# Row tiles of the first token group in two runs of three, and low parts one product later, in a one-core attention, MLP and mixture kernel

## The chip, the cores and the metric

One core of a Trainium2 chip runs the whole program. The metric is the device time of one execution in microseconds (us). Engine names are those of the profile: PE is TensorE's matmul side, PEld its weight loads, DVE is VectorE, ACT is ScalarE, POOL is GpSimd, and SP issues the transfers.

## What is computed

Attention between 4 x 8 heads of 512 tokens and 32 state rows makes 2176 rows of 512 numbers. A leaky MLP follows (512 to 2048 to 512), and then eight experts, all of them applied to all rows and weighted by a matrix P, which a softmax over the gate and eight normalisations of rows and columns make:

```python
P = np.exp(logits - logits.max())
for _ in range(8):
    P /= P.sum(1, keepdims=True) + 1e-09
    P /= P.sum(0, keepdims=True) + 1e-09
    P *= N / E
for e in range(E):
    h = np.maximum(x @ w1[e], 0.0)
    ye = h @ w2[e]
    out += P[:, e:e + 1] * ye
```

Everything is float32. A float32 product is made of three fp32r products: high by high, high by low and low by high part.

## The kernel before

The change lies in the experts. `experts()` walks through 97 stages `s`: three token groups (768, 768 and 640 rows) times 32 units of 256 hidden columns (8 experts of 4 units), and one stage more to finish. In the first group, stage `s` makes two things.

The first is the first expert layer of unit `s`, as one level of Strassen's method: seven products, in the order m1, m6, m5, m7, m2, m4, m3 (the list that `quad` returns). Each is six matmuls of 128x384 into one of three PSUM banks, which the profile calls px (m1, then m2 on top), py (m6, then m7 and m4 on top) and pz (m5, then m3 on top). The banks come from a pool of three, so the next stage's m1, m6 and m5 write where this stage's px, py and pz were read. After m1, ACT copies px to p1. DVE adds (L956) make u2 from m6, u3 and c22 from m7, c21 from m4 and c12 from m3; c11 is px itself after m2. From each of the four results ACT makes a rectified high part (`g2h`, L971), and DVE the low part from the result and that high part (`g2l`, L972).

The second is the second expert layer of unit `s - 1`: six plain row tiles T0 to T5 of 128 tokens (`layer2_moe`), each six matmuls of 128x512 (L1267) into one of three banks, which DVE adds to the output rows, weighted by P (L1291; L1280 and L1285 in the first expert). T0 to T2 read the high and low parts of c11 and c21, T3 to T5 those of c22 and c12.

Every engine runs its instructions in the order in which this code issues them: the order of PE, DVE, ACT and SP in this part is the order of the text (`manual_schedule`). Other work comes in between at fixed places. `slot()` stands behind each product and each tile and lets the lanes advance: the splits of the next weights (ACT and POOL), the sums of the second layer's weights, which later groups need and which are written to DRAM (`sums_b`: L786, L789, L791, L794 on DVE, then two high parts L891 on ACT and two low parts L893 on DVE), the same sums of six units whose time is not at their own stage (lane "apart", input `rwl`), and the sums of the next group's rows (L697). `point()` counts places, and some lanes advance at listed counts (`PLACES`). In stages 1 to 5 the lane "gate" makes the normalisations of P: a chain of nine small DVE instructions (L513 to L516, L504 to L508) and a small PE product (pcs, L511), by turns.

`experts()` is also where the low parts are put: `relu` does not issue them, but appends them to the list `later`. Before the change a tile T follows product `min(T + lag, 6)`, with lag 1 (3 in stage 1), and `later` is emptied behind a tile's DVE instruction, from product 2 on (those of stage 0 behind the second product of stage 1).

Of the kernel before, what the change touches and what calls it, by code (L numbers as in the profile page):

```python
# [92 lines left out]
def body(ctx: ExitStack, tc: tile.TileContext, xt_in, xn_in, stb, stk, wd, ws, alpha, wgate, out):  # L93
# [589 lines left out]
    def sums_of(g):  # L683

        b11, b21, b12, b22 = blocks_of(g)
        t = {}
        homes = {1: (("T1 T2", "xl3"), ("T3", "xh4"), ("T4", "xl4")), 2: (("T1 T2", "xh4"), ("T3 T4", "xl4"))}
        for names, tag in homes[g]:
            names = names.split()
            rest = big.tile([P, len(names), 2, CH[2 * g][1]], F32, tag=tag, name=f"s{tag}_{g}")  # L690
            t |= {x: rest[:, i] for i, x in enumerate(names)}
        sum_t[g] = t
        for out, x, y in (
            (t["T1"], b12, b11), (t["T2"], b22, t["T1"]), (t["T3"], b22, b12), (t["T4"], b21, t["T2"])
        ):
            for k in range(2):
                nc.vector.tensor_tensor(out=out[:, k], in0=x[:, k], in1=y[:, k], op=ALU.subtract)  # L697
                yield 6
# [31 lines left out]
    def forms_in(made, names):  # L730
        for name in names.split():
            lanes["sums" if name in ("T1", "T2", "T4") else "blocks"].append(made[name])
# [64 lines left out]
    def weights_a(s):  # L797

        u = s % U2
        wa = [wp.tile([P, 3, FU], F32R, tag=f"wa{x}", name=f"wa{x}_{s}") for x in "hl"]  # L800
        wsum = [wp.tile([P, 4, FU], F32R, tag=f"ws{x}", name=f"ws{x}_{s}") for x in "hl"]
        pairs = [[w[:, i:i + 2, :] for w in wsum] for i in (0, 2)]
        name_left(left, s, wa, pairs)
        if s >= U2:
            for x, w, t in zip("hl", wa, wsum, strict=True):
                again(("a", x, u), w)
                again(("as", x, u), t)
            return
        t = raw2["a", s]
        if s == 0:  # L810
            sums = rawp.tile([P, 4, FU], F32, tag="raw", name=f"sum{s}")
        else:
            sums = p2["t"].tile([P, 4, FU], F32, tag="y", name=f"sum{s}", bufs=1)
        make = sums_left(nc.gpsimd, sums, *(t[:, i, :] for i in range(4)))
        yield next(make)
        split2(*wa, t[:, 0:3, :])
        for x, w in zip("hl", wa, strict=True):
            keep(("a", x, u), 0, 3, w)
        yield next(make) + 1
        split2(*pairs[0], sums[:, 0:2, :])  # L820
        yield 1
        split2(*pairs[1], sums[:, 2:4, :])
        for x, w in zip("hl", wsum, strict=True):
            keep(("as", x, u), 0, 4, w)
        if "raw" in p2:
            load_a(s + 1, p2["raw"])
        yield 1
# [86 lines left out]
    def apart():  # L914

        load_apart(None)
        yield 16
        for u in APART:
            yield from sums_b(u, raw_apart[u], "xl4", 4, 14)
# [247 lines left out]
    def finish(g):  # L1167

        yield 20
        yield from combine(g, nc.gpsimd, 14)  # L1170
        for h in range(2):
            for t0, nt in cuts(g, h):
                ps = rows(g, h, t0, nt)
                yield 1
                t = const.tile([P, DM], F32, tag="lt", name=f"row{g}_{h}_{t0}", bufs=1)
                nc.scalar.activation(out=t[:nt], in_=ps[:nt], func=AF.Copy)
                store(g, h, t0, nt, t)
                yield 5
# [56 lines left out]
    def spread_p():  # L1235

        for g in range(1, NG):
            t0, nt = GT[g]
            row = const.tile([E, 2 * CH[0][1]], F32, tag="lt", name=f"prow{g}", bufs=1)
            for i in range(0, nt, 3):  # L1240
                k = min(3, nt - i)
                ps = ps_a.tile([E, 512], F32, tag="a", name=f"ppr{g}_{i}")
                for j in range(k):
                    nc.tensor.transpose(ps[:, j * P:(j + 1) * P], pr[:, t0 + i + j, :], ident)
                yield 1
                nc.scalar.activation(out=row[:, i * P:(i + k) * P], in_=ps[:, :k * P], func=AF.Copy)
                yield 1
            spread[g] = dram.tile([E, 2 * CH[2 * g][1]], F32, tag=f"spread{g}", name=f"spread{g}")
            nc.sync.dma_start(out=spread[g], in_=row[:, :nt * P])
            yield 4  # L1250

    def load_p(g, e):

        n = 2 * CH[2 * g][1]
        nc.sync.dma_start(out=pb[:, e % 2, :n], in_=spread[g][e:e + 1, :].to_broadcast([P, n]))
# [48 lines left out]
    later, soon, lanes = [], [], {"gate": [], "early": [], "sums": [], "blocks": [], "w": [], "w2": [], "apart": [], "spread": [], "h": [], "out": []}  # L1304
    wait = dict.fromkeys(lanes, 0)

    def advance(lane):

        q = lanes[lane]
        while q:  # L1310
            try:
                wait[lane] = next(q[0]) - 1
                return True
            except StopIteration:
                q.pop(0)
        return False
# [4 lines left out]
    def point():  # L1321
        points[0] += 1
        for lane, at in at_point.items():
            while at and at[0] <= points[0] and advance(lane):
                at.pop(0)
# [22 lines left out]
    def flush(lane):  # L1348
        while advance(lane):
            pass  # L1350
        wait[lane] = 0
# [94 lines left out]
    def experts():  # L1446

        nonlocal pb, pool_order
        after = ["B11", "T2", "T1", "T3", "B21", "T4", "B22"]
        for s in range(NS2 + 1):  # L1450
            mults = quad(s) if s < NS2 else []
            plain = range(GT[0][1]) if 1 <= s <= U2 else []
            if s == UE + 2:
                lanes["apart"].append(apart())
            if s == U2 // 2:
                lanes["spread"].append(spread_p())
            if s == U2 - 5:
                flush("apart")
            if s % U2 == (U2 - 5 if s < U2 else U2 - 6) and s + U2 < NS2:
                lanes["early"].append(sums_of(s // U2 + 1))  # L1460
            if s % U2 == U2 - 1:
                flush("early")
                flush("spread")
            if s == U2:
                pool_order = tc.manual_schedule(engines={mybir.EngineType.Pool})
                pool_order.__enter__()
            if s == U2 + 1:
                banks.close()
                p2["m"] = ctx.enter_context(tc.tile_pool(name="ps_m", bufs=2, space=PSUM))
                p2["tr"] = ctx.enter_context(tc.tile_pool(name="ps_t", bufs=1, space=PSUM))  # L1470
            if s + 1 < NS2:
                lanes["w"].append(weights_a(s + 1))
            if s < NS2:
                lanes["w2" if s > 1 else "w"].append(weights_b(s))
            made = forms(s // U2 + 1) if s % U2 == U2 - 1 and s + 1 < NS2 else None
            if U2 < s < NS2:
                lanes["h"].append(sums2(s - 1))
            if s == 2 * U2 + 1:
                lanes["out"].append(finish(1))

            lag = 3 if s == 1 else 1

            for i in range(7):
                if i == 3 and s == U2 - 1:
                    pb = big.tile([P, 2, 768], F32, tag="xl5", name="pb")
                if i == 3 and s % UE == UE - 1 and U2 - 1 <= s < NS2 - 1:
                    load_p((s + 1) // U2, (s + 1) % U2 // UE)
                if mults:
                    point()
                    mults[i]()  # L1490
                    if made:
                        forms_in(made, after[i])
                    if i == 1:
                        while later:
                            later.pop(0)()
                    slot()
                for t in plain:
                    if min(t + lag, 6) == i:
                        point()
                        layer2_moe(s - 1, t)  # L1500
                        while later and i > 1:
                            later.pop(0)()
                        slot()
                if U2 < s < NS2:
                    product(s - 1, i)
                    slot()
            for lane in ("w", "w2", "sums", "blocks"):
                flush(lane)
        flush("out")
        finish_last(NG - 1)  # L1510
        pool_order.__exit__(None, None, None)
# [66 lines left out]
```

## Time and profile before

| What | Value |
|---|---|
| device time, median of 3 runs | 1783.4 us (1783.14 to 1783.88) |
| span of the profiled execution, first to last instruction | 1781.5 us |
| PE busy in the span | 1755.4 us, 99% |
| DVE busy in the span | 1511.1 us, 85% |
| POOL, ACT busy in the span | 1254.5 us, 714.5 us |
| granted TensorE clock, mean | 0.998 of full speed |

The span is the profiled execution's own time; what lies around it shows only in the runs' median, which is 1.9 us more. A share is a mean over stages with different limits, so the stretch of the first token group (about 403 to 908 us) is read by itself below. A busy PE is a modelled figure: matmuls are pipelined, and what tells a full PE from a waiting one is the distance from one matmul's start to the next one's.

### The profile page before, as it was taken

The numbers are of one execution on the slowest core, as the hardware profiler recorded it, in microseconds if no ns is written. First come the engines' busy times: TensorE is split into PE (matmuls) and PEld (weight loads), VectorE is DVE, ScalarE is ACT, GpSimd is POOL, SyncE is SP. The second block draws the span as 40 slices with busy tenths as digits, with TensorE's granted clock in tenths as the row PEclk, the third lists the DMA queues.
The fourth block names the chain that finished last, engine by engine and source line by source line (L and its number), as shares of the span: only waits on it lengthen the run. The fifth ranks groups of instructions, "written<-read, shape, count | busy, mean of one in ns | idle before, by whom it ended". The sixth has DMA issues, their size and how long they took to land.

```text
span 1781.5 us, 28789 instructions
## 1 busy us (share of the span) xinstructions
PE 1755.4 (99%) x9963; PEld 1637.0 (92%) x9963; DVE 1511.1 (85%) x2349; ACT 714.5 (40%) x1350; POOL 1254.5 (70%) x1288
## 2 busy tenths in 40 slices
PE   8999999999999999999999999999999999999998
PEld 8888888878888888888899999999998999999998
DVE  7879878778999999999977777777888888778877
ACT  7747667553334444443422222222223323233332
POOL 4536546577588777778657777777777897677775
PEclk9999999999999999999999999999999999999999
DMA  6212111227688999988877776777776887888884
GB/s 219 83 54 72 36 59 48 77 86 251 213 320 305 341 343 334 345 322 295 324 287 260 263 258 254 263 265 263 255 263 237 308 300 286 308 321 294 308 313 155
DMA packets 153009, 427.18 MB, mean 240 GB/s; under 512 B 17296, under 2 KB 34192, under 8 KB 152864
## 3 DMA queue, kind: packets, MB, share of 16 engines
q1 hardware_dynamic: 152864, 425.34, 66.3%
q8 instruction: 80, 1.31, 0.3%
q14 instruction: 65, 0.53, 0.1%
HBM read 302.28 MB, written 122.99 MB: 239 GB/s over the span
## 4 chain that ended last, share of the span: by engine, by line
PE 87%; DVE 8%; ACT 2%; POOL 2%; issue 1%; DMA 0%; SPq 0%; DVEq 0%; POOLq 0%; ACTq 0%
PE pm L1122 23%; PE py L949 15%; PE po L1267 13%; PE pz L949 10%; PE px L949 10%; PE po L634 7%; PE ph L602 4%; PE pv L528 1%; DVE g2l L972 1%; PE psr L382 1%; DVE acc L647 1%; DVE raw L173 0%; POOL xg L410 0%; DVE al L541 0%; PE psc L304 0%
## 5 line engine op out<-in xcount | busy, mean ns | idle before, releaser
L1128 DVE TENSOR_TENSOR m<-pm,m 128x768 f32<-128x768 f32 (+1 forms) x427 | 377.6, 886 | 126.8 <-PE pm L1122 126.8
L1122 PE MATMUL pm<-formgh,wz 128*128 128x384 f32 (+1 forms) x1134 | 213.4, 323 | 0.4 <-DVE m L1128 0.4
L1053 POOL TENSOR_TENSOR formgh<-mid,formgh 128x384 fp32r<-128x384 f32 (+1 forms) x126 | 121.2, 962 | 107.2 <-ACT formgh L1052 107.1
L949 PE MATMUL px<-rB,wah 128*128 128x384 f32 (+1 forms) x768 | 188.1, 327 | 1.3 <-DVE g2l L972 1.3
L1122 PEld LDWEIGHTS pm<-formgh,wz 128*128 128x128 f32 x1134 | 187.5, 189 | 0.7 <-issue 0.7
L949 PE MATMUL py<-rT,wsh 128*128 128x384 f32 (+1 forms) x768 | 187.6, 326 | 0.0
L758 POOL TENSOR_TENSOR w2l<-rw,w2h 128x512 fp32r<-128x512 f32 x64 | 86.0, 1366 | 112.6 <-ACT w2h L756 101.9
L971 ACT ACTIVATE g2h<-c 128x384 fp32r<-128x384 f32 x96 | 50.5, 526 | 284.9 <-DVE c L956 271.7
L1267 PE MATMUL po<-w2l,g2h 128*128 128x512 f32 x384 | 152.4, 397 | 0.0
L1267 PE MATMUL po<-w2h,g2h 128*128 128x512 f32 x384 | 151.6, 395 | 0.0
L1267 PE MATMUL po<-w2h,g2l 128*128 128x512 f32 x384 | 149.7, 390 | 0.0
L949 PEld LDWEIGHTS px<-rB,wah 128*128 128x128 f32 x768 | 135.9, 188 | 7.7 <-DVE g2l L972 2.1
L1063 POOL TENSOR_TENSOR T<-mid,mid 128x384 f32<-128x384 f32 (+1 forms) x126 | 118.0, 959 | 30.8 <-DVE mid L1037 30.0
L949 PEld LDWEIGHTS py<-rT,wsh 128*128 128x128 f32 x768 | 135.9, 188 | 2.9
L1052 ACT ACTIVATE formgh<-mid 128x384 fp32r<-128x384 f32 (+1 forms) x126 | 63.0, 500 | 179.4 <-DVE mid L1037 136.0
L1291 DVE SCALAR_TENSOR_TENSOR oa<-po,pr,oa 128x512 f32<-128x512 f32 x168 | 124.3, 740 | 11.7 <-PE po L1267 10.8
L616 POOL TENSOR_TENSOR gl<-r,gh 128x512 fp32r<-128x512 f32 x64 | 88.0, 1385 | 58.2 <-ACT gh L120 36.6
L1037 DVE SCALAR_TENSOR_TENSOR mid<-mid,pb 128x384 f32<-128x384 f32 (+1 forms) x192 | 121.9, 635 | 6.6
L1122 PE MATMUL pm<-formgl,w2h 128*128 128x384 f32 (+1 forms) x504 | 121.1, 323 | 4.1 <-POOL formgl L1053 2.2
L949 PE MATMUL px<-rB,wal 128*128 128x384 f32 (+1 forms) x384 | 125.2, 326 | 0.0
L949 PE MATMUL py<-rT,wsl 128*128 128x384 f32 (+1 forms) x384 | 125.1, 326 | 0.0
L1063 POOL TENSOR_TENSOR formgl<-T,formgl 128x384 fp32r<-128x384 f32 (+1 forms) x126 | 120.9, 959 | 1.2 <-ACT formgl L1070 1.2
(260 smaller groups left out, 5039.5 us busy)
## 6 DMA issues: line engine op xcount, KB each, us to landing
wz<-kept_bs SPq DMA_DIRECT2D x126, 512.0 KB, 8.1
kept_bs<-wz SPq DMA_DIRECT2D x64, 512.0 KB, 5.7
wsh<-kept_as_h SPq DMA_DIRECT2D x64, 512.0 KB, 3.8
wsl<-kept_as_l SPq DMA_DIRECT2D x64, 512.0 KB, 6.0
wah<-kept_a_h SPq DMA_DIRECT2D x64, 384.0 KB, 3.0
wal<-kept_a_l SPq DMA_DIRECT2D x64, 384.0 KB, 4.4
w2h<-kept_b_h SPq DMA_DIRECT2D x63, 384.0 KB, 6.3
w2l<-kept_b_l SPq DMA_DIRECT2D x63, 384.0 KB, 6.9
```

Source lines behind the costliest of these rows:

```text
L602: nc.tensor.matmul(ps, lhsT=w, rhs=x, start=(i == 0), stop=(i == len(terms) - 1))
L616: nc.gpsimd.tensor_tensor(out=lo, in0=r, in1=f32(hi), op=ALU.subtract)
L634: nc.tensor.matmul(bank, lhsT=w, rhs=x, start=first_of, stop=last_of)
L758: nc.gpsimd.tensor_tensor(out=lo[:, i], in0=src[:, i], in1=f32(hi[:, i]), op=ALU.subtract)
L949: nc.tensor.matmul(bank[b], lhsT=w[:, k * P:(k + 1) * P], rhs=xf[:, j, k, :], start=(first and i == 0), stop=(i == 5), skip_group_check=True,)
L1037: nc.vector.scalar_tensor_tensor(out=out, in0=src, scalar=0.0, in1=pb[:, e % 2, h * n:(h + 1) * n], op0=ALU.max, op1=ALU.mult)
L1053: nc.gpsimd.tensor_tensor(out=lo, in0=out, in1=f32(hi), op=ALU.subtract)
L1063: nc.gpsimd.tensor_tensor(out=out, in0=x, in1=y, op=ALU.subtract)
L1122: nc.tensor.matmul(ps[:, q, :n], lhsT=w[:, q * P:(q + 1) * P], rhs=x, start=(j == 0), stop=(j == 2))
L1128: nc.vector.tensor_tensor(out=mm[g][name], in0=ps[:, :, :n], in1=mm[g][name], op=ALU.add)
L1267: nc.tensor.matmul(ps, lhsT=x[:, f, t * P:(t + 1) * P], rhs=w[:, f, :], start=(i == 0), stop=(i == 3 * NF - 1))
L1291: nc.vector.scalar_tensor_tensor(out=a, in0=ps, scalar=p, in1=a, op0=ALU.mult, op1=ALU.add)
```

## The change

The tiles no longer stand one behind each product. T0 to T2 follow product 1 (m6) and T3 to T5 product 4 (m2); in stage 1 they follow products 4 and 6. The list `later` is taken at each product: what has been appended up to then is issued behind that product's own instructions. Behind a tile `later` is emptied in any case. No instruction is added or taken away in the first group's arithmetic, and the later groups have neither tiles nor such low parts.

```diff
-            lag = 3 if s == 1 else 1
+            tiles_after = {4 if s == 1 else 1: (0, 1, 2), 6 if s == 1 else 4: (3, 4, 5)}
 
             for i in range(7):
...
                 if mults:
                     point()
+                    due = list(later)
+                    later.clear()
                     mults[i]()
+                    for fn in due:
+                        fn()
                     if made:
                         forms_in(made, after[i])
-                    if i == 1:
-                        while later:
-                            later.pop(0)()
                     slot()
                 for t in plain:
-                    if min(t + lag, 6) == i:
+                    if t in tiles_after.get(i, ()):
                         point()
                         layer2_moe(s - 1, t)
-                        while later and i > 1:
+                        while later:
                             later.pop(0)()
                         slot()
```

The order on the engines shows what moves. The first place is DVE in the middle of stage 22, around the result c22 of product m7 (`sumb22` are the sums of the stage's weights, `po2_21_2` is tile T2 of unit 21, `g2l` a low part). Before:

```order
L956 TENSOR_TENSOR u3_22_7899<-py22_7829,p1_22_7812 128x384
L956 TENSOR_TENSOR c22_22_7901<-pz22_7856,u3_22_7899 128x384
L794 TENSOR_TENSOR sumb22_7854<-rw2_22_7736,sumb22_7854 128x256
L1291 SCALAR_TENSOR_TENSOR oa0_4065<-po2_21_2_7907,pr_96,oa0_4065 128x512
L972 SCALAR_TENSOR_TENSOR g2l22_7803<-c22_22_7901,g2h22_7802 128x384
L893 TENSOR_TENSOR wz_22_0_7918<-sumb22_7854,wz_22_0_7918 128x512
```

And now, the same engine and place:

```order
L791 TENSOR_TENSOR sumb22_7854<-rw2_22_7735 128x256
L794 TENSOR_TENSOR sumb22_7854<-rw2_22_7735,sumb22_7854 128x256
L956 TENSOR_TENSOR u3_22_7910<-py22_7829,p1_22_7811 128x384
L956 TENSOR_TENSOR c22_22_7912<-pz22_7894,u3_22_7910 128x384
L972 SCALAR_TENSOR_TENSOR g2l22_7802<-c22_22_7912,g2h22_7801 128x384
L893 TENSOR_TENSOR wz_22_0_7917<-sumb22_7854,wz_22_0_7917 128x512
```

A sum and the addition of T2 stood between c22 and its low part; now nothing does, and the low part still needs the high part that ACT makes of c22.

The second place is DVE at the end of stage 21 and the start of stage 22 (`wz_4_0` belongs to the lane "apart"). Before:

```order
L956 TENSOR_TENSOR c21_21_7769<-py21_7649,p1_21_7632 128x384
L893 TENSOR_TENSOR wz_21_1_7761<-sumb21_7674,wz_21_1_7761 128x512
L1291 SCALAR_TENSOR_TENSOR oa0_4065<-po2_20_4_7774,pr_96,oa0_4065 128x512
L972 SCALAR_TENSOR_TENSOR g2l21_7624<-c21_21_7769,g2h21_7623 128x384
L956 TENSOR_TENSOR c12_21_7789<-pz21_7676,u2_21_7656 128x384
L1291 SCALAR_TENSOR_TENSOR oa0_4065<-po2_20_5_7793,pr_96,oa0_4065 128x512
L972 SCALAR_TENSOR_TENSOR g2l21_7624<-c12_21_7789,g2h21_7623 128x384
L893 TENSOR_TENSOR wz_4_0_7734<-sumb4_7434,wz_4_0_7734 128x512
```

And now:

```order
L1291 SCALAR_TENSOR_TENSOR oa0_4082<-po2_20_4_7763,pr_96,oa0_4082 128x512
L893 TENSOR_TENSOR wz_21_1_7761<-sumb21_7674,wz_21_1_7761 128x512
L1291 SCALAR_TENSOR_TENSOR oa0_4082<-po2_20_5_7773,pr_96,oa0_4082 128x512
L956 TENSOR_TENSOR c21_21_7787<-py21_7649,p1_21_7631 128x384
L956 TENSOR_TENSOR c12_21_7797<-pz21_7710,u2_21_7656 128x384
L972 SCALAR_TENSOR_TENSOR g2l21_7623<-c21_21_7787,g2h21_7622 128x384
L893 TENSOR_TENSOR wz_4_0_7733<-sumb4_7432,wz_4_0_7733 128x512
L972 SCALAR_TENSOR_TENSOR g2l21_7623<-c12_21_7797,g2h21_7622 128x384
```

The result c21 stood ahead of the second weight sum and of two tile additions; it now stands behind them, and c12 and the two low parts follow it closely.

The third place is PE across the border of stages 21 and 22 (the first matmuls of each piece; the rest repeat it). Before, from m4 (py21) on:

```order
L949 MATMUL py21_7649<-rT4_0_3712,wah_21_7459 128x384 x2
...
L949 MATMUL pz21_7676<-rB22_0_3641,wsh_21_7461 128x384 x2
...
L1267 MATMUL po2_20_5_7793<-w2h_20_7466,g2l20_7447 128x512
...
L949 MATMUL px22_7805<-rB11_0_3469,wah_22_7635 128x384 x2
...
L949 MATMUL py22_7829<-rT2_0_3639,wsh_22_7637 128x384 x2
...
L1267 MATMUL po2_21_0_7846<-w2h_21_7642,g2l21_7624 128x512
```

And now, from the last tile ahead of m4 on:

```order
L1267 MATMUL po2_20_5_7773<-w2h_20_7466,g2l20_7446 128x512
...
L949 MATMUL py21_7649<-rT4_0_3712,wah_21_7459 128x384 x2
...
L949 MATMUL pz21_7710<-rB22_0_3641,wsh_21_7461 128x384 x2
...
L949 MATMUL px22_7804<-rB11_0_3469,wah_22_7635 128x384 x2
...
L949 MATMUL py22_7829<-rT2_0_3639,wsh_22_7637 128x384 x2
...
L1267 MATMUL po2_21_0_7846<-w2h_21_7642,g2l21_7623 128x512
```

Between m4 and the next stage's m6, which takes m4's bank, stood T4, m3, T5 and m1; now m3 and m1 stand there.

## Rows read from the trace of the kernel before

**Rows 1.** The page: busy time by engine, and DVE in 40 slices.

```profile
PE 1755.4 (99%) x9963; PEld 1637.0 (92%) x9963; DVE 1511.1 (85%) x2349; ACT 714.5 (40%) x1350; POOL 1254.5 (70%) x1288
...
DVE  7879878778999999999977777777888888778877
```

**Rows 2.** The timeline of PE, stage 21: start us, length us.

```profile
720.68 0.51 PE L949 MATMUL px<-rB,wah 128*128 128x384 f32 x2
...
722.77 0.39 PE L1267 MATMUL po<-w2h,g2l 128*128 128x512 f32 x1
...
736.32 0.51 PE L949 MATMUL px<-rB,wah 128*128 128x384 f32 x2
```

**Rows 3.** Windows of the first group: stretch, its length, each engine's busy us.

```profile
464.60:500.31 35.71, 32.82 (x160) 27.88 (x158) 34.52 (x60) 11.77 (x21) 23.45 (x26) 1.00 0.69 240
500.31:673.51 173.20, 173.20 (x867) 155.43 (x868) 171.90 (x255) 72.05 (x131) 137.22 (x144) 1.00 0.91 331
673.51:767.60 94.09, 94.09 (x471) 84.48 (x470) 87.91 (x134) 39.42 (x71) 73.23 (x79) 1.00 0.92 335
767.60:830.16 62.56, 62.56 (x313) 56.23 (x312) 60.01 (x93) 25.76 (x46) 48.84 (x52) 1.00 0.88 322
830.16:877.08 46.92, 46.92 (x235) 42.17 (x234) 46.39 (x70) 18.39 (x33) 33.81 (x35) 1.00 0.79 283
```

**Rows 4.** The timeline of PE's weight loads: in brackets idle us before, and releaser.

```profile
477.57 0.30 PEld L949 LDWEIGHTS py<-rT,wah 128*128 128x128 f32 x2 [1.64 <-DVE u L956]
...
500.31 0.30 PEld L949 LDWEIGHTS px<-rB,wah 128*128 128x128 f32 x2 [1.25 <-DVE g2l L972]
```

**Rows 5.** The timeline of DVE, stage 21.

```profile
724.36 0.75 DVE L1291 SCALAR_TENSOR_TENSOR oa<-po,pr,oa 128x512 f32<-128x512 f32 x1 [0.77 <-PE po L1267]
...
729.23 0.56 DVE L956 TENSOR_TENSOR c<-pz,u 128x384 f32<-128x384 f32 x1
729.71 0.60 DVE L794 TENSOR_TENSOR sumb<-rw,sumb 128x256 f32<-128x256 f32 x1
...
730.90 0.54 DVE L972 SCALAR_TENSOR_TENSOR g2l<-c,g2h 128x384 fp32r<-128x384 f32 x1
...
733.64 0.54 DVE L956 TENSOR_TENSOR c<-py,p 128x384 f32<-128x384 f32 x1
734.11 1.04 DVE L893 TENSOR_TENSOR wz<-sumb,wz 128x512 fp32r<-128x512 f32 x1
735.07 0.74 DVE L1291 SCALAR_TENSOR_TENSOR oa<-po,pr,oa 128x512 f32<-128x512 f32 x1
735.73 0.54 DVE L972 SCALAR_TENSOR_TENSOR g2l<-c,g2h 128x384 fp32r<-128x384 f32 x1
```

**Rows 6.** The timeline of ACT, the high parts of c22 and c21.

```profile
729.88 0.53 ACT L971 ACTIVATE g2h<-c 128x384 fp32r<-128x384 f32 x1 [4.75 <-DVE c L956]
...
734.22 0.53 ACT L971 ACTIVATE g2h<-c 128x384 fp32r<-128x384 f32 x1 [1.61 <-DVE c L956]
```

**Rows 7.** The timeline of PE, stage 1: three tiles on end.

```profile
411.25 0.39 PE L1267 MATMUL po<-w2h,g2l 128*128 128x512 f32 x1
...
412.64 0.39 PE L1267 MATMUL po<-w2h,g2l 128*128 128x512 f32 x1
...
414.01 0.39 PE L1267 MATMUL po<-w2h,g2l 128*128 128x512 f32 x1
```

**Rows 8.** The timeline of DVE, end of stage 2: a gate chain, first and last.

```profile
432.66 0.15 DVE L513 TENSOR_SCALAR cb<-pcs 128x8 f32<-128x8 f32 x1
...
434.80 0.42 DVE L508 TENSOR_REDUCE cs<-pr 128x8 f32<-128x136 f32 x1
```

**Rows 9.** DVE by line and form, 500.31 to 673.51 us: busy us, mean ns.

```profile
L789 DVE TENSOR_TENSOR sumb<-sumb,rw 128x256 f32<-128x256 f32 x11 | 15.4, 1401 | 0.4
...
L791 DVE TENSOR_TENSOR sumb<-rwl 128x256 f32<-128x256 f32 x4 | 1.6, 408 | 0.0
```

**Rows 10.** The timeline of POOL, stage 21: four splits on end.

```profile
728.41 3.63 POOL L758 TENSOR_TENSOR wsl<-sum,wsh 128x256 fp32r<-128x256 f32 x4
```

## Prediction

> **What bounds the kernel now.** The page comes first: PE is busy for 99% of the span, DVE for 85%, but DVE's slices stand at nine tenths from the eleventh to the twentieth, which is the first token group, the only place that the change touches [rows 1]. There PE's timeline gives the length of a stage: from one m1 to the next 15.64 us, with 2.09 us for m1 and m6, so 1.04 us a product, and 1.39 us a tile [rows 2, 7]; 7 x 1.04 + 6 x 1.39 = 15.62, so in such a stage PE never waits. The windows show both engines. From 500 to 674 us (stages 7 to 17) PE is full, and DVE is idle for 1.3 of 173.2 us; in stages 28 to 30 for 0.5 of 46.9; in stages 18 to 27 for 8.7 of 156.7 [rows 3]. So PE sets the time, but DVE runs level with it, and where it fell behind, in stages 5 and 6, PE lost 2.9 of 35.7 us [rows 3] in waits of m4 for u3 and of m1 for a low part [rows 4]. The question is thus whether the new order makes DVE wait: what DVE loses in stages 5 to 17, PE loses.
>
> **What the new order adds on DVE.** No instruction is added, so the cost lies in waits.
>
> First, the low part of c22. Before, a sum and T2's addition stand between c22 and its low part, 1.67 us from start to start [rows 5], and ACT's high part ends within that time [rows 6]. Now the low part is next. c22 starts at 729.23, frees DVE for the next instruction at 729.71, and ends at 729.79 [rows 5]; ACT starts 0.09 us later and takes 0.53 [rows 6], so the high part ends at 730.41. DVE stands for 0.70 us at least; with a handover as long as the longest that I read, 0.21 us from a product's end to DVE, 0.91. I take 0.75, as the handover from DVE to ACT took 0.09. Behind it in DVE's queue stand the weight sums' low part, T3, and all that follows.
>
> Second, the end of the stage. c21 and c12 now stand together, then their two low parts. c21 frees DVE 0.47 us after its start, and its high part ends 1.11 us after it (733.64 to 734.75 [rows 5, 6]); c12 fills 0.47 of the 0.64 between. That leaves 0.2 to 0.35, and I take 0.25. Together 1.0 us a stage.
>
> A rule of the Trainium skill speaks against the change here: its page PSUM — Partial Sum Buffer, section Engine vs sequencer instructions, says that VectorE's queue is strictly first in, first out. By that rule the 1.0 us is lost whole; if ready instructions could pass a waiting one, it would be nothing. The trace agrees as far as it goes: DVE stood for 0.77 us for T0's product with the weight sums queued behind it [rows 5].
>
> **What it adds on PE.** m6 overwrites the bank that c21 is read from. Between m4's end and the next m6 there were 4.86 us (T4, m3, T5, m1); now 2.08 (m3, m1). Take the loop through it. From c21's end: about 0.1 us, m6 1.04, T0 1.39, and 0.2 until DVE adds T0, 2.7 together. From T0's addition to c21's end DVE now does what stood between these two before, 724.36 to 734.18 or 9.82 us, and also the second weight sum's low part (0.96), T4's and T5's additions (0.66 each) and the 0.75 of waiting [rows 5]: 12.85. The loop is 15.6 against PE's 15.64: a plain stage just fits, and each further DVE piece between T0 and c21 goes straight onto PE. In the first 2.7 us of the loop DVE has only c12, two low parts and u2, about 2.1 with the 0.25; where no lane's piece lies there, 0.6 is lost as well.
>
> **The sum.** Where lane pieces stand I read from the order of the changed program.
>
> In stages 7 to 17: 11 x 1.0 = 11.0. A sum covers the first wait in stage 10 (-0.75), and pieces between c21 and c12 the second in four stages (-1.0). DVE's present 1.3 us of idle time goes: 7.95. Five stages (7, 8, 11, 12, 14) have nothing in the first 2.7 us: + 5 x 0.6 = 3.0. That is 11.0.
>
> In stages 5 and 6: 2.0, less 0.75 where a sum covers it: 1.25, of which idle time could hide all; since PE waits there already, I take 1.2.
>
> In stages 18 to 23: 6.0 - 5 x 0.25 = 4.75, against 6.2 of idle time, but in a loop with 0.04 to spare: 0 to 1, taken 0.5. Stages 24 to 27: 4.0 - 1.5 - 0.25 = 2.25, against 2.55: 0. Stages 28 to 30: 3.0 - 0.25, less 0.5 idle, is 2.2, and 0.6 in two of them: 3.4.
>
> In stages 2 and 4 a gate chain, 2.56 us [rows 8], now stands between c21 and c12, ahead of c21's low part, which T0's fourth matmul needs. m4's end to c21's end 0.8, chain 2.56, c12 0.47, low part 0.54: 4.4, against 3 x 1.04 + 3 x 0.23 = 3.8 on PE: 0.5 each, 1.0.
>
> PE's gain: a tile behind a tile took 1.37, not 1.39 [rows 7]; four a stage in 31 stages is 2.5, but it counts only where PE doesn't wait, in some 13 of them: -1.0.
>
> Together 11.0 + 1.2 + 3.9 + 1.0 - 1.0 = 16.1. It stands on a span of 1781.5, with 1.9 around it to the runs' median of 1783.4: 1799.5 us.
>
> **What could shift the sum.** The weight sums take 1.40 us where the same shape takes 0.41 from the other lane [rows 9], so DVE's own durations move with what runs beside them. One sum a stage that falls into a quiet place gives back 1.0; one more that doesn't costs as much. If the 0.6 were lost in all 24 stages from 7 to 30 and not in 7, it would be 10 more: 1810.
>
> The page SBUF — State Buffer, section Who interferes with whom, says that a DVE instruction with two SBUF inputs is held up by a GpSimd instruction that reads SBUF. By it each low part that moves could lose up to one POOL split, 0.9 us, 28 us over stages 1 to 31 for one a stage; the row shows a low part at 0.54 us under POOL's four splits, 728.41 to 732.04 [rows 5, 10], so by the row nothing. What that rule would bring is the third rival below, and more.
>
> **Rivals.** The first: the waits are paid for by shorter sums (no change). The tile additions, which read PSUM, now separate the sums, and POOL can run between them. It decides from 1.0 us a stage, where the four sums and two low parts have some 2.5 to give back. Against it: the last two sums now stand together, so that what one gains the next may lose. 1781 to 1786.
>
> The second: PE gains (faster). m4 now has 5.2 us after m7 for u3 and not 3.8, and the 2.9 us of waits in stages 5 and 6 go [rows 3, 4], with the 2.5 of the tiles: 1783.4 - 5.4 = 1778. It decides where DVE has 1.0 us idle in every stage; from 500 to 674 it has 0.12 [rows 3].
>
> The third: the bank of m6 and T0's low part hold PE in each stage (larger). DVE never gets ahead, and stages 18 to 27, too, lose 1 us: 10 more, and the 10 above: 1810 to 1820.
>
> **Numbers.** The forecast has 0.68, with its own range 1789 to 1811; no change 0.13, faster 0.10, larger 0.09. The range that holds 8 in 10 reaches from 1783 to 1815. 0.2% of 1783.4, 3.6 us, is what a measurement can tell from no change: faster 0.10, same 0.12, slower 0.78.
>
> **What will show it.** Right, if DVE shows idle time of about 0.7 us ahead of the low part of c22, released by ACT's L971, and PE's weight loads wait ahead of m6 (py from rT and wsh, behind px) for c21's addition, in stages 5 to 17 above all; stages 7 to 17 last 184 us and not 173; PE's distance within tiles and products, and all behind 908 us but the shift, stay as they are. Wrong, if DVE's low part waits and PE doesn't: then the sums got shorter. Wrong also if PE's waits are at T0's fourth matmul and not at m6: then the low parts' place, not the bank, is the price.

## The result, and the profile after

The changed kernel takes 1796.7 us (median of 4 runs, 1795.02 to 1798.56), the kernel before 1783.64 us in the same session: a ratio of 1.0071, 95% interval [1.0059, 1.0084]. That is 13.1 us slower, inside the forecast (1799.5 us, 1789 to 1811). The profiled span is 1793.2 us.

The page of the changed kernel, its busy times and DVE in 40 slices; [rows 1] are those of before.

```profile
PE 1758.0 (98%) x9963; PEld 1637.9 (91%) x9963; DVE 1492.2 (83%) x2349; ACT 712.1 (40%) x1350; POOL 1244.8 (69%) x1288
...
DVE  7879878778888989999977777777888887878877
```

DVE is busy for 18.9 us less than in [rows 1], although it runs the same 2349 instructions, and where before every slice from the eleventh to the twentieth stood at nine, four now stand at eight: the waits that the forecast expected, and shorter instructions that it did not.

Windows of the changed kernel, cut at the same stages as [rows 3]: stages 2 to 4, 5 and 6, 7 to 17, 18 to 23, 24 to 27, 28 to 30, 31 and 32. The first number behind the stretch is its length; the pairs after it are busy us and instructions of PE, PEld, DVE, ACT and POOL, then the granted clock.

```profile
415.21:465.57 50.36, 49.01 (x249) 43.58 (x248) 44.39 (x99) 14.27 (x25) 31.64 (x39) 1.00 0.60 222
465.57:506.79 41.22, 35.02 (x160) 29.96 (x160) 36.23 (x63) 12.12 (x22) 22.75 (x26) 0.92 0.64 228
506.79:683.24 176.45, 174.14 (x869) 155.34 (x868) 157.92 (x253) 70.99 (x130) 132.09 (x143) 1.00 0.88 320
683.24:777.65 94.41, 93.97 (x472) 84.58 (x472) 86.27 (x134) 38.74 (x71) 70.79 (x79) 1.00 0.89 328
777.65:841.30 63.65, 62.77 (x313) 56.25 (x313) 59.27 (x93) 25.42 (x46) 48.62 (x53) 1.00 0.88 321
841.30:891.12 49.82, 47.46 (x235) 42.14 (x235) 45.44 (x71) 18.16 (x33) 32.48 (x35) 1.00 0.77 278
891.12:922.27 31.15, 31.15 (x157) 28.18 (x157) 23.03 (x37) 10.73 (x18) 10.07 (x7) 1.00 0.91 324
```

Against [rows 3], stages 5 and 6 grew most, by 5.5 us, and in these two alone the granted clock is below full (0.92). The long stretch 7 to 17 grew by 3.2 us, and DVE is busy there for 157.9 us and not 171.9, with two instructions fewer inside the stretch (x253, x255).

The chain of waits, stages 7 to 30 of the changed kernel: who waits for whom, us in total, times, the longest.

```profile
DVE g2l L972 <- ACT g2h L971: 14.8, 23, 0.7
...
DVE oa L1291 <- PE po L1267: 14.3, 35, 0.8
...
PE py L949 <- DVE c L956: 6.0, 12, 1.4
```

The first row is c22's low part waiting for ACT's high part: 0.64 us in 23 of 24 stages. The last is m6 waiting for c21. Of the kernel before the same stretch lists neither.

The timeline of PE at the start of stage 11 shows one such wait: px from rB is m1, py from rT and wsh is m6.

```profile
571.22 0.51 PE L949 MATMUL px<-rB,wah 128*128 128x384 f32 x2
571.57 0.34 PE L949 MATMUL px<-rB,wal 128*128 128x384 f32 x1
572.14 0.59 PE L949 MATMUL py<-rT,wsh 128*128 128x384 f32 x2 [0.23 <-DVE c L956]
```

m6 starts 0.57 us behind m1's last matmul; inside a product the distance is 0.17. The 0.40 us between are the loss.

DVE by line and form in stages 7 to 17 of the changed kernel: busy us, mean ns, then idle us ahead and who ended it.

```profile
L972 DVE SCALAR_TENSOR_TENSOR g2l<-c,g2h 128x384 fp32r<-128x384 f32 x33 | 19.4, 604 | 8.5 <-ACT g2h L971 7.1
...
L794 DVE TENSOR_TENSOR sumb<-rw,sumb 128x256 f32<-128x256 f32 x11 | 10.5, 955 | 0.0
L791 DVE TENSOR_TENSOR sumb<-rw 128x256 f32<-128x256 f32 x11 | 9.1, 824 | 0.0
L789 DVE TENSOR_TENSOR sumb<-sumb,rw 128x256 f32<-128x256 f32 x11 | 6.9, 631 | 0.0
L786 DVE TENSOR_TENSOR sumb<-rw 128x256 f32<-128x256 f32 x11 | 6.6, 602 | 0.0
```

L789 took 1401 ns before [rows 9] and takes 631 now. The four sums together came to 3.99 us a stage before (1401, 1043, 943 and 603 ns for L789, L786, L791 and L794) and come to 3.01 now.

### The profile page after: what moved, and what is told of

The parts are those of the page before. It is cut to its first block, busy times and chain, and to the rows that moved or that the text cites. A ratio compares the mean times of both kernels' runs of the same rounds, so it can differ in the third digit from the quotient of the medians.

```text
span 1793.2 us, 28827 instructions
## 1 busy us (share of the span) xinstructions
PE 1758.0 (98%) x9963; PEld 1637.9 (91%) x9963; DVE 1492.2 (83%) x2349; ACT 712.1 (40%) x1350; POOL 1244.8 (69%) x1288
## 4 chain that ended last, share of the span: by engine, by line
PE 76%; DVE 13%; issue 3%; POOL 3%; ACT 2%; DMA 2%; SPq 1%; DVEq 0%; POOLq 0%; ACTq 0%
PE pm L1122 23%; PE py L949 13%; PE pz L949 8%; PE po L1267 8%; PE px L949 8%; PE po L634 7%; PE ph L602 4%; DVE oa L1291 2%; DMA rw<-in_ws_dram 1%; DVE wz L893 1%; DVE c L956 1%; PE pv L528 1%; POOL w2l L758 1%; DVE g2l L972 1%; PE psr L382 1%
```

## The experiments

Stretches are compared between profiled executions. The medians of before that ran beside them lay between 1783.18 and 1783.85 us.

**A sum over the wait.** The changed kernel, with the fourth sum between c22 and its low part:

```diff
         eng.tensor_tensor(out=s3, in0=a11, in1=a21, op=ALU.subtract)
         if gap:
-            yield gap
+            yield gap + (gap == 1)
```

> The changed kernel, but the last of the four weight sums of a stage goes one slot later, so that it stands on DVE between c22 and the low part of c22 and fills the time in which ACT makes the high part. Theory A (DVE's wait ahead of that low part is what PE pays for, through c21 and m6's bank): in the first group DVE's idle time ahead of low parts, released by ACT's high parts, falls from 18.0 us to under 6; PE's waits of m6 for c21 fall from 8.3 us to under 4; stages 7 to 30 get 4 to 7 us shorter; 1789 to 1793 us. Rival B (the 2.1 us between m4 and the next m6 are too short whatever DVE waits for): DVE's wait vanishes, m6's waits stay above 7 us, 1795 to 1798.

Measured: 1790.74 us, ratio 1.0042 [1.0029, 1.0054]. The waits of stages 7 to 30, and the window of 7 to 17:

```profile
DVE g2l L972 <- ACT g2h L971: 1.8, 8, 0.3
...
PE py L949 <- DVE c L956: 0.4, 1, 0.4
```

```profile
508.16:681.46 173.30, 172.89 (x868) 155.52 (x868) 155.87 (x254) 71.30 (x130) 131.78 (x143) 1.00 0.90 325
```

DVE's wait goes, and m6's wait with it, though m6 stands as close behind m4 as in the changed kernel. Stages 7 to 30 last 376.6 us (384.3 in the changed kernel, 376.8 before). What is left of the loss lies in stages 2 to 6, 6.3 us.

**The low parts' place alone.** The tiles as before, and `later` taken at each product:

```diff
+                    due = list(later)
+                    later.clear()
                     mults[i]()
+                    for fn in due:
+                        fn()
...
-                        while later and i > 1:
-                            later.pop(0)()
```

> The kernel before with one part of the change: each low part behind the next product, the tiles one behind each product as before. Theory A (the tile runs take away what covered c22's low part and shorten the way from m4 to m6; the place of low parts alone costs little, since a tile's addition still stands between c22 and its low part): 1782 to 1786 us, m6 waits for c21 under 1 us, the second weight sum still at 1.4 us. Rival C (the low parts' place is the price): 1790 us or more.

Measured: 1783.99 us, ratio 1.0 [0.9991, 1.0009], every stretch within 0.3 us of before. The low parts' place costs nothing by itself. (In this run no low part is issued behind a tile; in the changed kernel some are. The other half of the change, runs of three with the low parts in their old place, was not run.)

**Pairs.** The tiles in three runs of two, low parts as before:

```diff
-            lag = 3 if s == 1 else 1
+            tiles_after = {4: (0, 1), 5: (2, 3), 6: (4, 5)} if s == 1 else {1: (0, 1), 3: (2, 3), 5: (4, 5)}
```

> The kernel before with tiles in three runs of two, behind m6, m7 and m4, and low parts as before, behind tiles. Theory A: each of the three banks' readers has a run beside it again (2.8 us in runs between m6 and m7, between m7 and m4, and between m4 and the next m6), no wait of m6 for c21, and a plain stage lasts 15.59 instead of 15.64 us: 1780 to 1783.5 us. Rival D (any grouping of tiles makes DVE late, as its additions come in bursts): 1787 us or more, with PE waits in stages 7 to 17.

Measured: 1787.55 us, ratio 1.0023 [1.0013, 1.0032]. The time is that of rival D. An undisturbed stage stayed at 15.64 us, so two tiles on end gain nothing. But stages 7 to 17 grew by 2.6 us in three stages only (7, 8 and 14), so grouping does not make DVE late everywhere, and PE's form in that stretch names another wait at m6: a low part (of c11, from px), which now stands behind T4.

```profile
L949 PE MATMUL py<-rT,wsh 128*128 128x384 f32 x88 | 22.6, 337 | 1.7 <-DVE g2l L972 1.7
```

**From stage 7 on, and from stage 5 on.** Both keep the order before up to a stage and use the new one behind it:

```diff
+            old = s <= 6    # in the second of the two: s <= 4
+            if old:
+                lag = 3 if s == 1 else 1
...
+            else:
+                tiles_after = {1: (0, 1, 2), 4: (3, 4, 5)}
```

> The changed kernel with the old order in stages 0 to 6, the new one from stage 7 on. Theory A (stages 5 and 6, with the halved clock behind their waits, and stages 2 to 4 pay 6.8 of the 13 us): 1788 to 1792 us, granted clock 1.00 in all windows of the first group. Rival E (what stages 5 and 6 don't pay as waits of PE they hand on as backlog to stage 7 and later): 1794 us or more.

Measured: 1790.83 us, ratio 1.0049 [1.0037, 1.0062]. Stages 2 to 6 are as before, 7 to 17 last 177.3 us, 18 to 30 207.8: the loss behind stage 6 is not carried in from ahead of it.

> The order before in stages 1 to 4, the new order from stage 5 on. The changed kernel loses 5.5 us in stages 5 and 6 (41.2 and not 35.7), of which some 2.3 us are matmuls at the lower granted clock. If the order inside these two stages is the cause (they carry both a gate chain and the four sums, so DVE has nothing to give for its wait, and m6's bank passes it on), stages 2 to 4 last 49.0 us as before and stages 5 and 6 still 39 to 41.5; the whole is 1793 to 1796. If the loss was carried in from stages 2 to 4, where the gate chain holds c21's low part, stages 5 and 6 come back to 36 to 37.5 and the whole to 1789 to 1791.

Measured: 1795.48 us, ratio 1.0073 [1.0056, 1.0089]. Stages 2 to 4 last 49.05 us, stages 5 and 6 39.6 at a granted clock of 0.91. So most of that loss, 3.9 of 5.5 us, belongs to the order inside stages 5 and 6; 1.6 came with stages 2 to 4.

**T5 behind m3.** The changed kernel with one tile more between m4 and the next m6:

```diff
-            tiles_after = {4 if s == 1 else 1: (0, 1, 2), 6 if s == 1 else 4: (3, 4, 5)}
+            tiles_after = {4: (0, 1, 2), 6: (3, 4, 5)} if s == 1 else {1: (0, 1, 2), 4: (3, 4), 6: (5,)}
```

> The changed kernel with T5 behind m3 instead of behind T4 (stage 1 unchanged): between m4 and the next m6 stand m3, T5 and m1, 3.47 us and not 2.08, and DVE adds T5 behind c21 and not ahead of it. If m6's bank is where DVE's wait reaches PE, the waits of m6 (0.4 to 0.8 us each) go in stages 7 to 30 although DVE still waits 0.6 to 0.7 us ahead of c22's low part: 376 to 378 us in place of 384.3; the gate chain no longer stands between c21 and c12 in stage 2, and stages 5 and 6 last 36 to 38; the whole is 1783 to 1786. If DVE's lost time itself is the price, the wait only moves, to T0's fourth matmul (low parts of c21 and c12, now behind T5's addition) or to m4 (u3): 382 to 385 us, the whole about 1795.

Measured: 1788.34 us, ratio 1.0027 [1.0015, 1.0039]. The waits of stages 7 to 30:

```profile
DVE g2l L972 <- ACT g2h L971: 14.8, 23, 0.7
...
PE py L949 <- DVE c L956: 0.8, 3, 0.4
```

DVE waits for ACT exactly as long and as often as in the changed kernel, and m6's wait for c21 falls from 6.0 to 0.8 us: 378.1 us, and not 384.3 (376.8 before). DVE's wait alone costs little there; it becomes PE's through the bank. With the first run (the sum over the wait), each of the two causes has been taken away alone, and each time the loss behind stage 6 went, here but for 1.3 us. The whole is 2.3 us above the expectation, as stages 2 to 6 still last 86.9 us (84.7 before).

**Old order up to stage 6, the covered wait behind it.**

```diff
-            yield gap
+            yield gap + late    # late: 1 for these sums from unit 7 on
...
+            old = s <= 6
```

> The order before in stages 1 to 6, the runs of three from stage 7 on, and from stage 7 on the fourth sum one slot later, so that it stands between c22 and its low part. If the loss has two separate places (DVE's wait ahead of c22's low part in stages 7 to 30, and the crowded stages 2 to 6), both go: stages 2 to 6 last 84.7 us as before, stages 7 to 30 some 376 us, and the whole 1782 to 1784, within 0.1% of before. If instead the border between the two orders costs by itself (the variant with the new order from stage 7 lost 2 us in stage 8), stage 8 is long again and the whole is 1785 to 1786. Gain of tile behind tile, 0.07 us a stage: 24 x 0.07 = 1.7 us at the most.

Measured: 1783.74 us, ratio 0.9996 [0.9987, 1.0005]. Both places of loss are gone. An undisturbed stage is 15.57 us, but stages 8 and 14 last 16.53 and 16.12, so stages 7 to 30 come out at 377.3 and the tiles' gain is eaten.

**A tile between two sums.** The kernel before, with T1's addition between the first two sums:

```diff
         eng.tensor_tensor(out=s1, in0=a21, in1=a22, op=ALU.add)
         if gap:
-            yield gap
+            yield gap + (gap == 1)
         eng.tensor_tensor(out=s2, in0=s1, in1=a11, op=ALU.subtract)
-        yield 1
+        if gap != 1:
+            yield 1
```

> The kernel before with one pair exchanged on DVE: the second weight sum (L789) stands behind T1's addition and not ahead of it, so that T1 stands between the first two sums and L789 and L791 follow each other. If a sum is long because it stands right behind another sum, L789 falls from 1.40 to about 0.65 us in stages 7 to 17 and L791 rises from 0.94 to some 1.0: DVE gets 11 x 0.7 = 7.7 us idle there. PE is full there, so the stages stay at 173.2 us; stages 5 and 6 may fall from 35.7 to 33 to 35. The whole is 1781 to 1784. If the length goes by what POOL does at that time and not by the neighbour, L789 stays over 1.2 us or passes its length on to L791, and nothing changes.

Measured: 1792.96 us, ratio 1.0053 [1.004, 1.0065]. DVE's four sums by form in stages 7 to 17 (lines behind L789 count one more in this kernel):

```profile
L786 DVE TENSOR_TENSOR sumb<-rw 128x256 f32<-128x256 f32 x11 | 12.2, 1107 | 0.0
...
L792 DVE TENSOR_TENSOR sumb<-rw 128x256 f32<-128x256 f32 x11 | 10.5, 959 | 0.0
L789 DVE TENSOR_TENSOR sumb<-sumb,rw 128x256 f32<-128x256 f32 x11 | 9.3, 847 | 0.0
L795 DVE TENSOR_TENSOR sumb<-rw,sumb 128x256 f32<-128x256 f32 x11 | 6.6, 598 | 0.0
```

L789 fell by 0.55 us, not by 0.75, and the four come to 3.51 us: the neighbour accounts for half of the 0.98 us that the sums lost in the changed kernel. What made up the other half stays open. The time missed both expectations: stages 7 to 17 last 175.2 us (173.2 before), 18 to 23 96.9 (94.1 before), and stages 24 to 27 68.7 (62.6 before), where ACT's high part of a sum waits up to 7.2 us for a store (`kept_bs`) and m1's copy, which is queued behind it, comes late; why one place in DVE's order brings this about there was not followed up.

**Stages 5 and 6 without their sums, and without the scalings.** The first makes the high and low parts of units 5 and 6 from the weights as they are:

```diff
+        bare = gap == 1 and u in (4, 5, 6)    # unit 4 has no sums here
+        if bare:
+            sums = raw.rearrange("p f (b c) -> p (f b) c", c=FU)
+            yield 4
```

> The changed kernel without the four weight sums on DVE of units 5 and 6 (the high and low parts are made of the weights as they are, so the second layer of these two units in the later groups comes from other weights). DVE has 3.5 to 4 us less to do in each of stages 5 and 6. If DVE's backlog there makes PE's waits, and these waits the fall of the granted clock, then stages 5 and 6 last 32.5 to 35 us and not 41.2, the granted clock stays at 1.00 through them, stages 2 to 4 stay at 50.4, stages 7 to 17 at 176, and the whole is 1788 to 1791. If the clock falls for another reason it falls at the same place (near the first products of stage 6), and stages 5 and 6 last 37 or more.

Measured: 1804.85 us, ratio 1.0124 [1.0107, 1.0142]. Stages 5 and 6 last 38.1 us, with a granted clock of 0.74 and 0.50 at the first products of stage 6. For these two stages that is the second expectation: without the sums they are 3.1 us shorter than in the changed kernel, so the sums carry part of their length, but the clock falls all the same. (Stages 18 to 27 lost 9 us more in this kernel; not followed up.)

The timeline of DVE at the end of stage 5 of the changed kernel shows what else fills DVE there:

```profile
484.42 0.48 DVE L1290 TENSOR_SCALAR oa<-oa,pr 128x512 f32<-128x512 f32 x1
485.00 0.75 DVE L1291 SCALAR_TENSOR_TENSOR oa<-po,pr,oa 128x512 f32<-128x512 f32 x1
...
486.13 0.48 DVE L1290 TENSOR_SCALAR oa<-oa,pr 128x512 f32<-128x512 f32 x1
486.71 0.75 DVE L1291 SCALAR_TENSOR_TENSOR oa<-po,pr,oa 128x512 f32<-128x512 f32 x1
...
487.98 0.48 DVE L1290 TENSOR_SCALAR oa<-oa,pr 128x512 f32<-128x512 f32 x1
488.56 0.75 DVE L1291 SCALAR_TENSOR_TENSOR oa<-po,pr,oa 128x512 f32<-128x512 f32 x1
489.23 0.55 DVE L956 TENSOR_TENSOR c<-py,p 128x384 f32<-128x384 f32 x1
```

In stage 5 alone each tile's addition is preceded by a scaling of its output rows (L1290), six in all, 4.8 us; all six now stand ahead of c21 (the last row), for which m6 waits, where four did before. The second kernel leaves the scalings out:

```diff
             if t == 0:
                 flush("gate")
-            nc.vector.tensor_scalar(out=a, in0=a, scalar1=pr[:, tt, 0:1], scalar2=None, op0=ALU.mult)
```

> The changed kernel without the six scalings of the output rows by the first column of P (L1290, one ahead of each tile's addition in stage 5, 0.48 to 1.40 us each, 4.8 us in all), so the first expert stays unweighted in the output. If these pieces, three of which now stand ahead of c21, are what the forecast of stages 5 and 6 left out, then stages 5 and 6 last 35 to 37 us and not 41.2, the granted clock stays at 1.00 there, the other stretches stay as in the changed kernel (50.4, 176 to 177, 94, 64, 50), and the whole is 1790 to 1793. If the gate chain or the weight sums are the cause, stages 5 and 6 stay over 38 us and the clock falls as before.

Measured: 1790.02 us, ratio 1.0039 [1.0025, 1.0053]; windows of stages 2 to 4, 5 and 6, 7 to 17:

```profile
416.14:467.51 51.37, 50.05 (x254) 44.44 (x252) 45.49 (x101) 14.80 (x26) 31.64 (x39) 1.00 0.62 226
467.51:502.01 34.50, 32.19 (x160) 28.19 (x159) 31.79 (x57) 12.13 (x22) 23.92 (x26) 1.00 0.71 251
502.01:678.45 176.44, 174.12 (x868) 155.28 (x868) 158.17 (x253) 71.03 (x130) 132.11 (x143) 1.00 0.90 324
```

Stages 5 and 6 fall from 41.2 to 34.5 us, a little below the expectation, the clock stays at 1.00, and the rest is that of the changed kernel (the first row begins 1 us early, so that stretch is 50.4 too). The kernel before has the six scalings as well, and was not run without them; the nearest is the next run, the old order there with the scalings on ACT, at 33.9 us.

**The scalings on ACT.** The kernel of 1783.74 us, with L1290 moved:

```diff
-            nc.vector.tensor_scalar(out=a, in0=a, scalar1=pr[:, tt, 0:1], scalar2=None, op0=ALU.mult)
+            nc.scalar.activation(out=a, in_=a, func=AF.Copy, scale=pr[:, tt, 0:1])
```

> The variant with the old order up to stage 6, the runs of three from stage 7 on and the fourth sum one slot later there (1783.74 against 1783.67 us), with the six scalings of stage 5 (L1290) on ACT and not on DVE. ACT is idle for more than half of that stretch; a pass of 384 columns takes it 0.53 us, so I estimate 0.65 for 512. If the scalings are what fills DVE in stage 5, stages 5 and 6 fall from 35.1 to 31.5 to 33.5 us, stages 7 to 30 stay at 377, and the whole is 1780 to 1782.5, the first to beat both orders by more than 0.1%. If ACT, which has to wait for the end of the gate chain ahead of the first scaling, then delivers its high parts late, the waits come back at the low parts of stage 5 and nothing is won (1783 to 1785).

Measured: 1781.79 us, ratio 0.999 [0.9981, 0.9999]: less than the 0.2% that a measurement here tells from no change, though the interval ends below one. Stages 5 and 6 last 33.9 us (35.1 without the move), a little over the expectation; a scaling takes ACT 0.71 us, and DVE waits for it 3.4 us in all.

## Why the prediction was right, and where its sum was not

The time came out 2.8 us under the forecast, but two terms were wrong, in opposite directions: stages 7 to 17 lost 7.8 us less than their term, stages 5 and 6 lost 4.3 us more. That the total lies so near is luck.

| Term | Forecast | Stretch after less before |
|---|---|---|
| stages 2 and 4, gate chain | +1.0 | +1.3 (stages 2 to 4) |
| stages 5 and 6 | +1.2 | +5.5 |
| stages 7 to 17 | +11.0 | +3.2 |
| stages 18 to 23, 24 to 27, 28 to 30 | 0.5, 0, 3.4 | 0.3, 1.1, 2.9 |
| PE's gain, tile behind tile | -1.0 | in the rows above; 31 and 32: -0.1 |
| sum | 16.1 | 14.3 (medians: 13.1) |

The two profiled spans differ by 11.7 us only. Ahead of stage 2 the changed kernel's is 0.4 us shorter, and behind stage 32 it is 2.2: in the last 280 us the granted clock of the profiled execution of before is 0.99, that of the changed kernel 1.00.

**The first wait: right.** 0.75 us was taken for c22's low part; it is 0.64, and it stands in stage 10 too, where the forecast had a sum cover it. By the queue rule of the Trainium skill, PSUM — Partial Sum Buffer, section Engine vs sequencer instructions, what is queued behind the low part waits too, and the trace agrees as far as the order goes: in stage 5 the low part starts at 483.28 us after a wait of 0.65 us, and the weight sum's low part behind it at 483.81. The second wait, taken at 0.25 us, is 0.13 in stages 7 to 17 (L972's 8.5 us of idle time less 7.1 for ACT, over 11).

**The bank: right.** The waits are at m6, for c21, as the loop said, and the two runs that took DVE's wait or m6's closeness away each brought stages 7 to 30 back, to 376.6 and 378.1 us. At T0's fourth matmul, the other place named, PE waits where the gate chain stands between c21 and c12, as the third part of the sum had it. The timeline of PE, stage 3 of the changed kernel:

```profile
436.16 0.50 PE L1267 MATMUL po<-w2h,g2l 128*128 128x512 f32 x1 [1.32 <-DVE g2l L972]
```

That is the chain behind stage 2. The one behind stage 4 shows not in the row of stages 2 to 4 but in stage 5, where PE's product pcs waits 0.99 us for it (0.32 before).

**Stages 7 to 17: the loop right, the sum mis-sized.** By the loop a plain stage just fits, and each further DVE piece between T0 and c21 goes onto PE. The timeline of DVE bears that out; T0's addition and c21, in stage 7 and then in stage 8:

```profile
511.19 0.75 DVE L1291 SCALAR_TENSOR_TENSOR oa<-po,pr,oa 128x512 f32<-128x512 f32 x1 [0.43 <-PE po L1267]
...
524.09 0.54 DVE L956 TENSOR_TENSOR c<-py,p 128x384 f32<-128x384 f32 x1
...
527.49 0.75 DVE L1291 SCALAR_TENSOR_TENSOR oa<-po,pr,oa 128x512 f32<-128x512 f32 x1 [0.76 <-PE po L1267]
...
539.82 0.55 DVE L956 TENSOR_TENSOR c<-py,p 128x384 f32<-128x384 f32 x1
```

From T0's addition to c21 it is 12.90 us in stage 7 and 12.34 in stage 8. Read in the same way, it is 12.65 us or more in stages 6, 7, 10, 11, 13 and 14, and in the stage behind each of these m6 starts 0.4 to 0.8 us late; in stages 8, 9, 12, 15 and 16 it is 12.34 or less (11.7 and 11.8 in stages 9 and 16, where only the four sums and two low parts of sums lie there), and m6 is at most 0.1 us late. Windows of stages 7, 8, 9 and 14:

```profile
506.79:523.09 16.30, 15.81 (x79) 14.03 (x79) 14.71 (x25) 6.55 (x12) 11.13 (x13) 1.00 0.67 238
523.09:539.39 16.30, 15.82 (x79) 14.04 (x79) 14.37 (x24) 6.55 (x12) 13.03 (x14) 1.00 0.97 360
539.39:555.12 15.73, 15.73 (x79) 14.04 (x79) 13.80 (x23) 6.03 (x11) 12.02 (x13) 1.00 0.93 341
...
618.57:635.02 16.45, 15.83 (x79) 14.05 (x79) 15.18 (x25) 6.61 (x12) 11.86 (x13) 1.00 0.84 290
```

Stage 9 has 15.73 us, near the 15.57 of a stage without a wait; the other three have 16.3 to 16.5.

Of the 11.0 us, the step that failed is the 7.95, "DVE's present 1.3 us of idle time goes". It booked DVE's lost time on PE in all eleven stages, although by its own loop a plain stage loses nothing, and it held DVE's other durations fixed. DVE lost 8.5 us ahead of L972, but its work there became 14.0 us shorter (171.9 to 157.9; I estimate that 1.3 of it are the two instructions fewer), so it had time left over: it waited 9.1 us for tiles. That is the mechanism of the first rival, at some 1.2 us a stage against the 1.0 from which it was to decide, and still not its result, because a loop with a further piece does not fit. So the stretch came to 176.45 us, and not to the 184 that was named as a sign.

The 3.0 us for five stages (7, 8, 11, 12, 14) came to 2.9 in stages of these numbers, with 0.4 more in stage 15, but not for the reason given. The loops that begin behind c21 of these five, at the start of stages 8, 9, 12, 13 and 15, are those without a lane's piece ahead of T0's addition, and DVE does idle 0.76 us in each; of the stages that follow these starts (9, 10, 13, 14 and 16) only 14 lost more than 0.1 us. At the start of stages 7, 11 and 14 a lane's sums lie there, and m6 of the next stage was late all the same. What lies between T0's addition and c21 decided.

That the sums got shorter is shown; why is shown for half only (the tile between two of them).

**Stages 5 and 6: wrong in size.** The step took 1.0 us a stage as elsewhere and counted T4's and T5's additions at 0.66 us. It left out L1290, which the trace of before shows in these stages as well: the scalings belong to the tiles, and those of T4 and T5 move with them, ahead of c21. Without all six the stretch is 34.5 us. Some 2.3 of the 5.5 us are a second thing that the forecast had no term for, the clock (below). An estimate from these rows: two scalings of 0.48 us, 0.7 for the second gate chain and 2.3 for the clock are 4.0 of the 4.3 us by which the term was short.

**The gain: right in kind.** An undisturbed stage is 15.57 us, not 15.64. Pairs gave none of it.

**The other rivals.** Faster failed in stages 5 and 6, which got longer instead of freeing their 2.9 us. The larger loss did not come: low parts kept their length (604 ns, 614 before, for the form from c in stages 7 to 17), though by the rule of the Trainium skill, SBUF — State Buffer, section Who interferes with whom, each could have lost a split. The trace agrees with that rule in kind, which the forecast's single row did not show: low parts from c took 0.72 us on average where POOL was busy throughout (30 of 96 before; 0.78 for 24 of 96 now) and 0.55 where it was idle, and beside the low part of 0.54 us in that row one split took 1.16 us and the other three 0.74 to 0.93. Fewer of them run beside POOL now than before, so what that costs did not grow.

## What to carry to other kernels

A wait costs what the next reuse of a buffer cannot absorb: before moving work, count the producer's time up to the read that frees a bank and the consumer's time up to its next write, stage by stage, with every piece that rides along with the moved work, also those that exist in one stage only. The durations of DVE's sums were no constants (0.41 to 1.50 us for one shape); when the order around such instructions changes, a forecast needs a term for them. Where two conditions are needed for a loss, take each away alone: here one slot for a sum, or one tile, was enough.

## What was not expected of the hardware

The granted clock fell inside the first group. Windows of the changed kernel around the first products of stage 6; the third figure from the end is the clock:

```profile
486.00:488.00 2.00, 1.34 (x6) 1.01 (x6) 1.90 (x5) 0.00 (x0) 0.00 (x0) 1.00 0.29 117
488.00:490.00 2.00, 0.08 (x1) 0.11 (x1) 1.90 (x5) 0.19 (x1) 0.00 (x0) 0.50 0.60 227
490.00:492.00 2.00, 2.00 (x7) 2.00 (x8) 1.27 (x3) 2.00 (x4) 0.00 (x0) 0.50 0.93 295
492.00:494.00 2.00, 2.00 (x6) 1.61 (x5) 0.56 (x1) 1.89 (x4) 1.80 (x2) 0.50 0.46 172
494.00:496.00 2.00, 2.00 (x8) 1.60 (x8) 1.22 (x2) 0.00 (x0) 2.00 (x3) 0.79 0.48 179
```

PE had waited for m1 and then for m6, and went on at the lower of its two levels (1.2 and not 2.4 GHz) until 494.9 us. The timeline of PE there:

```profile
486.27 0.62 PE L949 MATMUL px<-rB,wah 128*128 128x384 f32 x2 [1.82 <-DVE g2l L972]
...
489.92 0.98 PE L949 MATMUL py<-rT,wsh 128*128 128x384 f32 x2 [2.31 <-DVE c L956]
...
491.98 0.63 PE L1267 MATMUL po<-w2h,g2l 128*128 128x512 f32 x1
...
494.54 0.53 PE L1267 MATMUL po<-w2h,g2l 128*128 128x512 f32 x1
```

m6 takes 2.06 us instead of 1.04, and T0 2.56 instead of 1.39: 2.2 us, and 0.1 more on T1, on top of the waits themselves. Before, PE waited in stages 5 and 6 as well [rows 4], and the clock stayed at 1.00 [rows 3]. Here two longer stalls close together cost 2.3 us more behind them, and without the scalings, with shorter stalls at the same places (0.18 and 1.14 us), nothing. One stall can do it too: with T5 behind m3, PE stood in stage 5 for the gate chain, and the windows 472 to 474 and 474 to 476 us have a clock of 0.63 and 0.52.

```profile
471.55 0.39 PE L511 MATMUL pcs<-cs,ones 128*128 128x8 f32 x2 [2.48 <-DVE cs L508]
```

And one sum of 128x256 took from 0.41 to 1.50 us in one and the same kernel, with the order of DVE's instructions and not their number deciding over some 13 us of DVE's time in eleven stages.
